# A retention and two-layer MoE kernel: earlier loads in layer 1's accumulators, units from step 4, output products behind the pair

## The chip, the cores and the metric

The kernel runs on one core of a Trainium2 chip. The time is device microseconds of one execution, and of several executions the median is given. The core's engines work side by side, each through its own queue in order: TensorE (PE, with its weight loads PEld), VectorE (DVE), ScalarE (ACT), GpSimd (POOL) and SyncE (SP, which issues most DMAs here).

## What is computed

Eight heads of retention over four batches of 576 tokens, then two dense layers with 2048 inner units over all 2304 tokens. Cut from the reference:

```python
scores = scale * np.matmul(q, k.transpose(0, 1, 3, 2))          # 4 x 8 heads, 576 x 576
gamma = 1.0 - 2.0 ** (-5.0 - np.arange(H, dtype=np.float32))
Dmat = np.where(rel >= 0, gamma[:, None, None] ** rel[None, :, :], 0.0)
attn_out = np.matmul(scores * Dmat[None], v)
x = attn_out.transpose(0, 2, 1, 3).reshape(B * S, H * D)         # 2304 x 512
h = x @ w_in;   x = np.maximum(0.01 * h, h) @ w_out              # layer 1
h = x @ w2_in;  x = (h - np.tanh(h)) @ w2_out                    # layer 2
```

The weights arrive as 64-bit floats.

## The kernel before

**Pairs.** The attention part (`retention`) goes over 16 pairs of heads (4 batches, 4 pairs each), numbered 0 to 15, two heads side by side on 128 partitions. The 576 tokens of a pair are four chunks of 128 and a tail of 64. For a pair, `prep` multiplies q and v with decay tables on POOL, `prep_tail` does the tail of q on VectorE and copies it into a block-diagonal tile `bd` on ScalarE; `scores` are k times q within each chunk (TensorE, into `sc`), `scores_tail` the same for the tail (`x_a`); `mask` applies the decay on VectorE and makes `pt`. `states_mm` makes k times v of each chunk (into `x_c`), and `states` runs the decayed sum over chunks into `st`: a copy on ScalarE and six operations on VectorE, each on the 64 partitions of one head, so that `st` is block-diagonal over 128 columns. One step later `outputs_far` multiplies `st` with q and `outputs_near` multiplies v with `pt`, both into the accumulator `o` and, for the tail, into a part of `x_c`; `finish` splits the result into a high half `xh` (ScalarE) and the rest `xl` (VectorE), which are layer 1's input.

**Narrow units.** Layer 1 begins inside the attention part. Its first group of four f-blocks is done for the first 1536 tokens in 12 units of 256 tokens and two f-blocks: `unit_h` (hidden product, 24 matmuls into `x_b`, then two activations `a` and `g` on ScalarE and a subtraction on POOL), `unit_o` (output product, 24 matmuls into `a`), `unit_evac` (into `acc`, after every second unit). The units' weights are the eight pieces of group 0. A piece is loaded raw (512 KB), narrowed from 64 to 32 bits by five operations (the first, `begin`, on ScalarE, then clamp, shift and two joins `top` and `low` on VectorE, into one of two buffers `cw`), and then split into two parts by `split_piece` (ScalarE, then POOL).

**What sets the order.** All is written in order by hand; each engine runs its own instructions in that order. Step i of the loop holds the load of pair i + 2, `prep` of pair i + 1, scores and mask of pair i, `prep_tail` of pair i + 1, then `pair_steps`. The piece operations are one list `ops`; `at_pair` says how many of them are done by the end of each step, and `fill` puts a third of a step's share at each of three places. SP issues pairs and pieces in the written order; a pair's tiles have three buffers, raw pieces two. In `pair_steps` before, from step 5 on (`first = NP + 1`), stand in a row: hidden product of unit u, output product of unit u - 1, far and near products of pair i - 1, states of pair i. After the loop the last hidden product and two output products follow. Then `layers` does the rest of both layers with `acc` as the accumulator of layer 1.

Of the kernel before, what the change touches and what calls it, by code (L numbers as in the profile page):

```python
# [10 lines left out]
F32 = mybir.dt.float32  # L11
# [22 lines left out]
def retention_moe_moe(  # L34
# [70 lines left out]
    def load_piece(key):  # L105
        m, kind, f = key
        src = ((w1i, w1o), (w2i, w2o))[m][kind][f]
        st = stage.tile([P, 512], I64 if wide else F32, tag="st", name="st")
        nc.sync.dma_start(out=st, in_=src)
        raw[key] = st  # L110
# [200 lines left out]
    def piece_ops(keys, split=True, spare=()):  # L311
# [3 lines left out]
        for j, key in enumerate(keys):  # L315
            part = narrow_ops(key)
            if j + 2 < len(keys):
                part.append(lambda k=keys[j + 2]: load_piece(k))
# [7 lines left out]
    def retention():  # L326
        with ExitStack() as ac:
# [18 lines left out]
            sts = [ak.tile([P, NFULL, P], F32, name=f"st{i}") for i in range(2)]  # L346
            bds = [ak.tile([P, 2, TAIL], F32, name=f"bd{i}") for i in range(2)]
            qk, kv, pts = {}, {}, {}
            order = [(b, p) for b in range(B) for p in range(NP)]

# [4 lines left out]
            def load_qk(i):  # L355
                b, p = order[i]
                t = ap_.tile([P, 2, S], F32, tag="qk", name="qk")
                nc.sync.dma_start(out=t[:, 1, :], in_=qT[b, p])
                nc.sync.dma_start(out=t[:, 0, :], in_=kT[b, p])
                qk[i] = t  # L360

            def load_v(i):
                b, p = order[i]
                t = ap_.tile([P, NFULL + NCH, P], F32, tag="kv", name="kv")
# [94 lines left out]
            def outputs_far(i):  # L459
# [300 lines left out]
```

## Time and profile before

| what | us |
|---|---|
| median of 3 runs (894.61 to 895.62) | 895.46 |
| span of the profiled execution | 893.7 |
| TensorE busy in that span | 868.6 (97%) |
| VectorE busy | 541.6 (61%) |
| ScalarE busy | 378.0 (42%) |
| POOL busy | 421.2 (47%) |
| end of the attention part (first matmul of `layers`) | 166.52 |

The median lies 1.76 us above the span of the profiled execution. The views that follow are stretches (busy time of each engine between two times), the chain of waits (followed back from the last instruction) and the timeline. TensorE's fp32 products appear as two records for each instruction. A form such as `64*128` behind a TensorE instruction is the part of the array, rows by columns, that it uses.

### The profile page before, as it was taken

The numbers are of one execution on the slowest core, as the hardware profiler recorded it, in microseconds if no ns is written. First come the engines' busy times: TensorE is split into PE (matmuls) and PEld (weight loads), VectorE is DVE, ScalarE is ACT, GpSimd is POOL, SyncE is SP. The second block draws the span as 40 slices with busy tenths as digits, with TensorE's granted clock in tenths as the row PEclk, the third lists the DMA queues.
The fourth block names the chain that finished last, engine by engine and source line by source line (L and its number), as shares of the span: only waits on it lengthen the run. The fifth ranks groups of instructions, "written<-read, shape, count | busy, mean of one in ns | idle before, by whom it ended". The sixth has DMA issues, their size and how long they took to land.

```text
span 893.7 us, 13252 instructions
## 1 busy us (share of the span) xinstructions
PE 868.6 (97%) x5024; PEld 747.0 (84%) x5024; DVE 541.6 (61%) x922; ACT 378.0 (42%) x767; POOL 421.2 (47%) x340
## 2 busy tenths in 40 slices
PE   6869999999999999999999999999999999999998
PEld 5759999988888889888888888888888888888886
DVE  6864544698898787865662544444545555555454
ACT  2333232232222321232324666675566555565553
POOL 4544342265223622264224654585457744585443
PEclk9789999999999999999999999999999999999999
DMA  7634432132365335631120200020001000001111
GB/s 276 230 124 131 137 107 101 48 118 95 132 186 166 107 118 157 186 106 47 48 83 24 61 12 1 0 72 24 1 1 43 17 1 1 1 1 48 48 48 70
DMA packets 28574, 70.95 MB, mean 79 GB/s; under 512 B 3296, under 2 KB 3680, under 8 KB 28512
## 3 DMA queue, kind: packets, MB, share of 16 engines
q1 hardware_dynamic: 27936, 69.74, 23.7%
q8 instruction: 39, 0.64, 0.3%
q10 hardware_dynamic: 576, 0.38, 0.1%
q14 instruction: 23, 0.19, 0.1%
HBM read 59.10 MB, written 11.01 MB: 78 GB/s over the span
## 4 chain that ended last, share of the span: by engine, by line
PE 92%; DMA 2%; DVE 2%; POOL 1%; ACT 1%; issue 1%; SPq 0%; POOLq 0%; ACTq 0%
PE h L194 40%; PE a L266 40%; PE a L543 4%; PE x_b L518 3%; DMA kv<-in_vn 2%; PE sc L401 1%; PE o L477 1%; PE o L465 1%; POOL wp L175 1%; PE x_c L434 1%; PE x_a L407 0%; POOL kv L378 0%; DVE cw L148 0%; DVE cw L142 0%; PE x_c L477 0%
## 5 line engine op out<-in xcount | busy, mean ns | idle before, releaser
L194 PE MATMUL h<-xh,wp 128*128 128x512 f32 (+1 forms) x1184 | 355.3, 366 | 0.0
L194 PEld LDWEIGHTS h<-xh,wp 128*128 128x128 f32 x1184 | 216.1, 188 | 36.9
L194 PE MATMUL h<-xl,wp 128*128 128x512 f32 (+1 forms) x592 | 216.9, 366 | 0.0
L266 PE MATMUL a<-wp,g 128*128 128x512 f32 x864 | 209.4, 390 | 0.2 <-POOL g L240 0.2
L266 PEld LDWEIGHTS a<-wp,g 128*128 128x128 f32 x864 | 161.0, 188 | 33.8 <-POOL g L240 1.0
L266 PE MATMUL a<-g,wp 128*128 128x512 f32 (+1 forms) x816 | 175.6, 364 | 0.0
L240 POOL TENSOR_TENSOR g<-v,g 128x512 fp32r<-128x512 f32 (+1 forms) x80 | 94.9, 1186 | 144.6 <-ACT g L239 144.5
L266 PEld LDWEIGHTS a<-g,wp 128*128 128x128 f32 x816 | 141.4, 189 | 24.6
L240 POOL TENSOR_TENSOR g<-a,g 128x512 fp32r<-128x512 f32 (+1 forms) x68 | 87.5, 1286 | 154.5 <-ACT g L208 141.1
L207 ACT ACTIVATE a<-h 128x512 f32<-128x512 f32 (+1 forms) x68 | 37.3, 548 | 227.1 <-PE h L194 226.1
L175 POOL TENSOR_TENSOR wp<-cw,wp 128x512 fp32r<-128x512 f32 x64 | 91.1, 1432 | 82.8 <-ACT wp L174 82.5
L194 PEld LDWEIGHTS h<-xl,wp 128*128 128x128 f32 x592 | 111.6, 189 | 18.6
L233 DVE TENSOR_TENSOR h<-h,t 128x512 f32<-128x512 f32 (+1 forms) x80 | 51.5, 644 | 107.3 <-ACT t L217 107.3
L148 DVE SCALAR_TENSOR_TENSOR cw<-st,cw 128x512 uint32<-128x512 uint32 x128 | 113.3, 885 | 4.0
L292 DVE TENSOR_TENSOR acc<-a,acc 128x512 f32<-128x512 f32 (+1 forms) x114 | 74.0, 662 | 68.3 <-PE a L266 68.1
L239 ACT ACTIVATE g<-v 128x512 fp32r<-128x512 f32 (+1 forms) x80 | 47.2, 589 | 145.4 <-DVE v L237 144.3
L218 POOL TENSOR_TENSOR v<-t,u 128x512 f32<-128x512 f32 (+1 forms) x80 | 94.7, 1184 | 14.2 <-ACT t L217 13.8
L234 DVE SCALAR_TENSOR_TENSOR v<-q,v 128x512 f32<-128x512 f32 (+1 forms) x80 | 55.5, 694 | 55.2 <-POOL v L218 54.2
L237 DVE COPY_PREDICATED v<-mk,h 128x512 f32<-128x512 uint32 (+1 forms) x80 | 54.8, 685 | 9.2 <-DVE v L234 1.4
L219 ACT ACTIVATE q<-u,qb 128x512 f32<-128x512 f32 (+1 forms) x80 | 54.5, 681 | 0.0
L222 ACT ACTIVATE mk<-u,qb 128x512 f32<-128x512 f32 (+1 forms) x80 | 54.2, 678 | 0.0
L131 DVE TENSOR_SCALAR cw<-st 128x512 uint32<-128x512 uint32 x56 | 40.5, 724 | 18.6 <-DMA st<-in_w2i 6.4
(60 smaller groups left out, 803.7 us busy)
## 6 DMA issues: line engine op xcount, KB each, us to landing
st<-in_w1i SPq DMA_DIRECT2D x16, 512.0 KB, 3.3
st<-in_w1o SPq DMA_DIRECT2D x16, 512.0 KB, 3.2
st<-in_w2i SPq DMA_DIRECT2D x16, 512.0 KB, 3.8
st<-in_w2o SPq DMA_DIRECT2D x16, 512.0 KB, 3.8
kept<-cw SPq DMA_DIRECT2D x24, 256.0 KB, 4.1
cw<-kept SPq DMA_DIRECT2D x24, 256.0 KB, 2.6
kv<-in_vn SPq DMA_DIRECT2D x16, 320.0 KB, 5.2
qk<-in_qT SPq DMA_DIRECT2D x16, 288.0 KB, 3.4
```

The lines of the kernel that those rows point to most:

```text
L148: nc.vector.scalar_tensor_tensor(out=t["w"], in0=t[src], scalar=scalar, in1=t["w"], op0=op, op1=ALU.bitwise_or)
L175: nc.gpsimd.tensor_tensor(out=wp[:, 1, :], in0=wf, in1=wp[:, 0, :].bitcast(F32), op=ALU.subtract)
L194: nc.tensor.matmul(out=ps[:, :n], lhsT=w[:, wi, cs], rhs=x[:, kk, t0:t0 + n], start=kk == 0 and i == 0, stop=kk == KK - 1 and i == 2,)
L218: nc.gpsimd.tensor_tensor(out=v[:, :n], in0=t_[:, :n], in1=u[:, :n], op=ALU.mult)
L219: nc.scalar.activation(out=q[:, :n], in_=u[:, :n], func=AF.Square, scale=math.sqrt(RHO_C), bias=qb[:, 0:1])
L222: nc.scalar.activation(out=mk[:, :n], in_=u[:, :n], func=AF.Relu, bias=qb[:, 1:2])
L233: nc.vector.tensor_tensor(out=h, in0=h, in1=t_, op=ALU.subtract)
L234: nc.vector.scalar_tensor_tensor(out=v, in0=q, scalar=RHO_A, in1=v, op0=ALU.add, op1=ALU.mult)
L237: nc.vector.copy_predicated(out=v, mask=mk.bitcast(U32), data=h)
L240: nc.gpsimd.tensor_tensor(out=gt[:, 1, :n], in0=v, in1=gt[:, 0, :n].bitcast(F32), op=ALU.subtract)
L266: nc.tensor.matmul(out=o, lhsT=l, rhs=r, start=f == 0 and i == 0 and d % pack == 0, stop=f == GF - 1 and i == 2 and (d + 1) % pack == 0, s ...
L292: nc.vector.tensor_tensor(out=dst, in0=a, in1=dst, op=ALU.add)
```

## The change

- `load_qk` and `load_v` put pairs 3 and 4 into parts of `acc` (table `homes`), and `load_piece` puts pieces 2 to 5 into other parts of it, so that all of these are queued ahead of the loop without waiting for a buffer. Pair j is then loaded in step i with j = i + 4 for i of 0 and 1 and i + 2 later, where j is over 4: pair 5 in step 1 and, by the same rule, again in step 3, each time into a fresh buffer.
- The pieces come in another order: both of `w_in`, both of `w_out`, for f-blocks 0 and 1, then the same for 2 and 3; `at_pair` is shorter.
- Units start in step 4 (`first = NP`). In `pair_steps` the far and near products of pair i - 1 and its `finish` come first, then the output product of unit u - 1, then the states of pair i, then the hidden product of unit u.
- `st` is 64 columns wide, with both heads on the 128 partitions; `states` is one copy and three operations with a column `decay` as factor; the far products are eight of 64 rows by 64 columns of the array in place of four of 128 by 128.

```diff
-    def load_piece(key):
+    def load_piece(key, at=None):
+        if at is None:
+            st = stage.tile([P, 512], I64 if wide else F32, tag="st", name="st")
+        elif wide:
+            st = acc[:, at:at + 1024].bitcast(I64)
...
-    def piece_ops(keys, split=True, spare=()):
+    def piece_ops(keys, split=True, spare=(), ahead=2):
-            if j + 2 < len(keys):
-                part.append(lambda k=keys[j + 2]: load_piece(k))
+            if j + ahead < len(keys):
+                part.append(lambda k=keys[j + ahead]: load_piece(k))
...
-            sts = [ak.tile([P, NFULL, P], F32, name=f"st{i}") for i in range(2)]
+            sts = [ak.tile([P, NFULL, 64], F32, name=f"st{i}") for i in range(2)]
+            decay = ak.tile([P, NP], F32, name="decay")
+            homes = {3: (4608, 5760), 4: (6912, 8064)}
...
-                for h in range(2):
-                    o = slice(64 * h, 64 * h + 64)
-                    nc.scalar.activation(out=st[o, 0, o], in_=c_[o, 0, :], func=AF.Copy)
+                nc.scalar.activation(out=st[:, 0, :], in_=c_[:, 0, :], func=AF.Copy)
                 for c in range(1, NFULL):
-                    for h in range(2):
-                        o = slice(64 * h, 64 * h + 64)
-                        nc.vector.scalar_tensor_tensor(
-                            out=st[o, c, o], in0=st[o, c - 1, o],
-                            scalar=float(gamma[2 * p + h] ** CH), in1=c_[o, c, :],
-                            op0=ALU.mult, op1=ALU.add,
-                        )
+                    nc.vector.scalar_tensor_tensor(
+                        out=st[:, c, :], in0=st[:, c - 1, :], scalar=decay[:, p:p + 1],
+                        in1=c_[:, c, :], op0=ALU.mult, op1=ALU.add,
+                    )
...
-                    nc.tensor.matmul(
-                        out=dst, lhsT=st[:, c - 1, :], rhs=q[:, cs],
-                        start=c in (1, NFULL), stop=False, skip_group_check=True,
-                    )
+                    for h in range(2):
+                        o = slice(64 * h, 64 * h + 64)
+                        nc.tensor.matmul(
+                            out=dst[o], lhsT=st[o, c - 1, :], rhs=q[o, cs],
+                            start=c in (1, NFULL), stop=False, skip_group_check=True,
+                        )
...
-            pieces = split_order(pieces_of(0, 0))
-            ops = piece_ops(pieces)
-            at_pair = [3, 8, 14, 21, 30, 44, 54]
-            first = NP + 1
+            pieces = [(0, kind, f0 + f) for f0 in (0, 2) for kind in range(2) for f in range(2)]
+            ops = piece_ops(pieces, ahead=6)
+            at_pair = [6, 12, 14, 18, 34, 50]
+            first = NP
...
-            def pair_steps(i, fast):
+            def pair_steps(i):
-                if fast:
-                    unit_h(u)
-                    fill(i, 1)
-                    if u:
-                        unit_o(u - 1)
-                        unit_evac(u - 1)
-                    u += 1
                 if i:
                     ot = outputs_far(i - 1)
                     outputs_near(i - 1, ot, [NFULL])
                     outputs_near(i - 1, ot, range(NFULL))
                     del pts[i - 1], kv[i - 1]
+                    finish(i - 1, ot)
+                if u:
+                    unit_o(u - 1)
+                    unit_evac(u - 1)
+                fill(i, 1)
                 if i < len(order):
                     states_mm(i)
-                if i:
-                    finish(i - 1, ot)
-                if i < len(order):
                     states(i)
+                    if i >= first:
+                        unit_h(u)
+                        u += 1
...
             load_v(0)
-            load_qk(1)
             load_piece(pieces[0])
-            load_v(1)
+            load(1)
+            load_piece(pieces[1])
+            load(2)
+            load(3)
+            load_piece(pieces[2], 0)
+            load_piece(pieces[3], 1024)
+            load(4)
+            load_piece(pieces[4], 2048)
+            load_piece(pieces[5], 3072)
...
-                if i + 2 < len(order):
-                    load(i + 2)
+                j = i + (2 if i > 1 else 4)
+                if 4 < j < len(order):
+                    load(j)
```

**TensorE in a full step, before** (`sc` scores, `x_a` their tail, `x_b` the hidden product, whose other rows are left out, `a` the output product, `o` and `x_c` far and near products, the last `x_c` the states):

```order
L401 MATMUL sc<-qk 128x128 x8
L407 MATMUL x_a<-bd_101,qk 128x128
L518 MATMUL x_b<-xh,wp 128x256
...
L543 MATMUL a<-g,wp 128x256 x24
L465 MATMUL o<-qk,st_100 128x128 x3
L465 MATMUL x_c<-qk,st_100 128x64
L477 MATMUL x_c<-pt,kv 64x64 x2
L477 MATMUL o<-pt,kv 64x128 x8
L434 MATMUL x_c<-kv 64x64 x8
```

**The same step in the changed kernel:**

```order
L420 MATMUL sc<-qk 128x128 x8
L426 MATMUL x_a<-bd_102,qk 128x128
L481 MATMUL o<-qk,st_100 64x128 x6
L481 MATMUL x_c<-qk,st_100 64x64 x2
L493 MATMUL x_c<-pt,kv 64x64 x2
L493 MATMUL o<-pt,kv 64x128 x8
L559 MATMUL a<-g,wp 128x256 x24
L453 MATMUL x_c<-kv 64x64 x8
L534 MATMUL x_b<-xh,wp 128x256
```

The output product now stands between the near products and the states, and the hidden product behind the states; the far products have twice the rows at half the output partitions.

**ScalarE in the step of the first unit, before** (step 5; `cw<-st` is a piece's first narrowing operation, `wp` its split, `bd` the tail copies, `xh` the finish, `st` the state copy, `a` and `g` the unit's two activations):

```order
L127 ACTIVATE cw<-st 128x512
L390 ACTIVATE bd_101<-qk 64x64 x2
L174 ACTIVATE wp<-cw 128x512
L525 ACTIVATE a<-x_b 128x512
L526 ACTIVATE g<-x_b 128x512
L127 ACTIVATE cw<-st 128x512
L174 ACTIVATE wp<-cw 128x512
L486 ACTIVATE xh<-x_c 128x64
L486 ACTIVATE xh<-o 128x512
L444 ACTIVATE st_100<-x_c 64x64 x2
```

**ScalarE in the step of the first unit in the changed kernel** (step 4; raw pieces are read from `acc`):

```order
L409 ACTIVATE bd_103<-qk 64x64 x2
L132 ACTIVATE cw<-acc 128x512
L179 ACTIVATE wp<-cw 128x512
L502 ACTIVATE xh<-x_c 128x64
L502 ACTIVATE xh<-o 128x512
L132 ACTIVATE cw<-acc 128x512
L461 ACTIVATE st_99<-x_c 128x64
L541 ACTIVATE a<-x_b 128x512
L542 ACTIVATE g<-x_b 128x512
L179 ACTIVATE wp<-cw 128x512
L132 ACTIVATE cw<-acc 128x512
```

The unit's two activations moved from ahead of the finish and the state copy to behind them, and a split and the next piece's first operation are queued behind the activations.

**SP's queue behind pair 3's load in the changed kernel** (`acc<-in_w` pieces 2 to 5, `acc<-in_q` pair 4, `st` pieces 6 and 7, `qk` and `kv` pair 5's two loads, the second one cut):

```order
L114 DMA acc<-in_w1o 128x512 x2
L370 DMA acc<-in_qT 128x576
L373 DMA acc<-in_kT 128x576
L384 DMA acc<-in_kn 128x512
L385 DMA acc<-in_vn 128x640
L114 DMA acc<-in_w1i 128x512 x2
L114 DMA st<-in_w1o 128x512
L370 DMA qk<-in_qT 128x576
L373 DMA qk<-in_kT 128x576
L384 DMA kv<-in_kn 128x512
L385 DMA kv<-in_vn 128x640
L114 DMA st<-in_w1o 128x512
```

Before, each piece from the third on stood behind one more pair, and both waited for a free buffer there.

## Rows read from the trace of the kernel before

**Rows 1.** Stretches: length; busy time (count) per engine; granted clock; DMA share, GB/s.
```profile
0.00:79.99 79.99, 58.84 (x608) 53.54 (x609) 55.32 (x140) 27.15 (x71) 37.82 (x33) 0.89 0.58 199
79.99:166.52 86.53, 86.53 (x964) 84.36 (x964) 36.18 (x115) 24.78 (x70) 29.24 (x23) 1.00 0.31 102
```

**Rows 2.** Chain of waits, one step: start us, duration us, engine, tile, line, records.
```profile
85.67 0.67 PE o L465 x6
86.51 0.27 PE x_c L477 x4
86.78 0.88 PE o L477 x16
87.65 0.46 PE x_c L434 x16
88.12 1.09 PE sc L401 x16
89.21 0.42 PE x_a L407 x2
89.63 2.87 PE x_b L518 x24
```

**Rows 3.** Chain of waits, the last step of the attention part.
```profile
155.64 3.06 PE x_b L518 x24
158.71 2.82 PE a L543 x24
...
163.50 3.02 PE a L543 x24
166.52 4.31 PE h L194 x36
```

**Rows 4.** Timeline of TensorE: start, duration, line, operands, array form, shape.
```profile
85.51 0.83 PE L465 MATMUL o<-qk,st 128*128 128x128 f32 x6
...
86.44 0.34 PE L477 MATMUL x_c<-pt,kv 128*64 128x64 f32 x4
...
88.05 1.16 PE L401 MATMUL sc<-qk 64*128 64x128 f32 x16
```

**Rows 5.** Timeline of VectorE: masks of pairs 1 and 4, state operations.
```profile
14.60 1.29 DVE L416 SCALAR_TENSOR_TENSOR pt<-sc,cm_sb 128x512 f32<-128x512 f32 x2
...
36.63 1.29 DVE L416 SCALAR_TENSOR_TENSOR pt<-sc,cm_sb 128x512 f32<-128x512 f32 x2
...
40.90 1.46 DVE L448 SCALAR_TENSOR_TENSOR st<-st,x_c 64x64 f32<-64x64 f32 x6
```

**Rows 6.** Stretches: the first loads, and the first hidden product.
```profile
4.00:14.00 10.00, 7.33 (x56) 6.41 (x57) 4.95 (x15) 1.61 (x6) 5.12 (x4) 1.00 1.01 373
...
39.83:44.08 4.25, 4.25 (x28) 4.25 (x28) 3.77 (x11) 1.42 (x4) 2.34 (x3) 0.70 0.63 227
```

**Rows 7.** Timeline of POOL: two operations that waited for a load to land.
```profile
12.56 1.26 POOL L378 TENSOR_TENSOR kv<-kv,vt_sb 128x640 f32<-128x640 f32 x1 [2.03 <-DMA kv<-in_vn]
...
14.63 1.28 POOL L373 TENSOR_TENSOR qk<-qk,qt_sb 128x512 f32<-128x512 f32 x1 [0.81 <-DMA qk<-in_qT]
```

**Rows 8.** Timeline: a narrowing shift while POOL works, and one without.
```profile
44.07 1.26 POOL L378 TENSOR_TENSOR kv<-kv,vt_sb 128x640 f32<-128x640 f32 x1 [1.87 <-PE x_b L518]
44.18 1.44 DVE L142 TENSOR_SCALAR cw<-cw 128x512 uint32<-128x512 uint32 x1
...
57.75 0.43 DVE L142 TENSOR_SCALAR cw<-cw 128x512 uint32<-128x512 uint32 x1
```

**Rows 9.** Timeline: activation, POOL's split of a unit, first narrowing operation, weight split.
```profile
49.06 0.59 ACT L526 ACTIVATE g<-x_b 128x512 fp32r<-128x512 f32 x1
49.83 1.31 POOL L527 TENSOR_TENSOR g<-a,g 128x512 fp32r<-128x512 f32 x1
49.91 0.68 ACT L127 ACTIVATE cw<-st 128x512 f32<-128x512 f32 x1 [0.27 <-POOL wp L175]
...
50.49 0.62 ACT L174 ACTIVATE wp<-cw 128x512 fp32r<-128x512 f32 x1
```

More of the change, by code (lines that the diff above doesn't have):

```diff
@@ L103, in retention_moe_moe @@
     early = [True]
-    def load_piece(key):
+    def load_piece(key, at=None):
         m, kind, f = key
         src = ((w1i, w1o), (w2i, w2o))[m][kind][f]
-        st = stage.tile([P, 512], I64 if wide else F32, tag="st", name="st")
+        if at is None:
+            st = stage.tile([P, 512], I64 if wide else F32, tag="st", name="st")
+        elif wide:
+            st = acc[:, at:at + 1024].bitcast(I64)
+        else:
+            st = acc[:, at:at + 512]
         nc.sync.dma_start(out=st, in_=src)
@@ L356, in load_qk @@
                 b, p = order[i]
-                t = ap_.tile([P, 2, S], F32, tag="qk", name="qk")
+                if i in homes:
+                    a = homes[i][0]
+                    t = acc[:, a:a + 2 * S].rearrange("p (s t) -> p s t", s=2)
+                else:
+                    t = ap_.tile([P, 2, S], F32, tag="qk", name="qk")
                 nc.sync.dma_start(out=t[:, 1, :], in_=qT[b, p])
+                if i == 0:
+                    nc.scalar.dma_start(out=qt_sb[:, 0, :], in_=qtab[:, 0, :])
                 nc.sync.dma_start(out=t[:, 0, :], in_=kT[b, p])
@@ L363, in load_v @@
                 b, p = order[i]
-                t = ap_.tile([P, NFULL + NCH, P], F32, tag="kv", name="kv")
+                n = NFULL + NCH
+                if i in homes:
+                    a = homes[i][1]
+                    t = acc[:, a:a + n * P].rearrange("p (c d) -> p c d", c=n)
+                else:
+                    t = ap_.tile([P, n, P], F32, tag="kv", name="kv")
                 nc.sync.dma_start(out=t[:, :NFULL, :], in_=kn[b, p])
@@ L574, in pair_steps @@
                     del pts[i - 1], kv[i - 1]
+                    finish(i - 1, ot)
[3 more added lines that the diff above has]
+                fill(i, 1)
                 if i < len(order):
                     states_mm(i)
-                if i:
-                    finish(i - 1, ot)
-                if i < len(order):
                     states(i)
-            t = ap_.tile([P, 2, S], F32, tag="qk", name="qk")
-            nc.sync.dma_start(out=t[:, 1, :], in_=qT[0, 0])
-            nc.scalar.dma_start(out=qt_sb[:, 0, :], in_=qtab[:, 0, :])
-            nc.sync.dma_start(out=t[:, 0, :], in_=kT[0, 0])
-            qk[0] = t
+                    if i >= first:
+                        unit_h(u)
+                        u += 1
+            load_qk(0)
             nc.scalar.dma_start(out=cm_sb, in_=cmask)
@@ L597, in retention @@
             nc.scalar.activation(out=qb[:, 3:4], in_=qb[:, 2:3], func=AF.Tanh)
-            for t in sts + bds:
+            for t in bds:
                 nc.vector.memset(t, 0.0)
-            load_piece(pieces[1])
+            for p in range(NP):
+                for h in range(2):
+                    nc.vector.memset(
+                        decay[64 * h:64 * h + 64, p:p + 1], float(gamma[2 * p + h] ** CH)
+                    )
             prep(0)
@@ L603, in retention @@
             for i in range(len(order)):
-                if i + 2 < len(order):
-                    load(i + 2)
-                fast = i >= first
+                j = i + (2 if i > 1 else 4)
+                if 4 < j < len(order):
+                    load(j)
                 if i + 1 < len(order):
@@ L614, in retention @@
                 fill(i, 0)
-                pair_steps(i, fast)
+                pair_steps(i)
                 fill(i, 2)
-            pair_steps(len(order), True)
+            pair_steps(len(order))
             assert done[0] >= len(ops)
-            unit_o(u - 1)
-            unit_evac(u - 1)
-            assert 2 * u == n_early
+            assert u == n_early // 2
     def layers():
```

## Prediction

> **What bounds the kernel now.** I read the stretches first. From 79.99 us to the end of the attention part at 166.52 us TensorE is busy 86.53 us of 86.53; in the 79.99 us ahead of that it is busy only 58.84 us, at a mean granted clock of 0.89 [rows 1]. After 166.52 us the MoE layers run as before, so the change can only move the moment at which the attention part ends. That moment is set by two things: when TensorE becomes saturated, and how much TensorE time is left then. The chain of waits prices the second, for one pair and one narrow unit [rows 2]: far products 0.67 + 0.17 us (85.67 to 86.51), near 0.27 + 0.88, states 0.46, scores 1.09, their tail 0.42, hidden product of a unit 2.87. The unit's output product takes 2.82 [rows 3]. One step is 9.65 us and nothing waits in it.
>
> **Part 1, units one step earlier.** In the changed kernel the first unit stands in step 4 instead of step 5, so when pair 8's scores are done one unit more is behind it, 5.69 us of TensorE time. I count from a place that both bounds can be tied to: the start of pair 6's scores, t6, which stands right behind the second unit's hidden product. Left from there in the changed order: 10 scores with tail (15.1), 11 far and near (21.9), 10 states (4.6), 10 hidden products (28.7), 11 output products (31.0), together 101.3 us at the prices of rows 2 and 3. So at unchanged prices the attention part would end level with before if t6 = 166.5 - 101.3 = 65.2.
>
> **Part 2, the output products later: form changes.** The profile prints for each TensorE instruction which part of the array it uses: near products and states `128*64`, scores `64*128`, tail, units and old far products `128*128` [rows 4]. Before, a step changes form three times: scores to tail, far to near, states to scores. What stands behind a change costs more than its columns. The tail is two passes that cost 0.11 each in the far products (0.67 for six) but it takes 0.42: 0.20 more. The scores take 1.09, where eight pairs of passes at 0.11 give 0.88: 0.21 more. The first four near passes, of 64 columns, take 0.27 behind the change, where sixteen of 128 columns take 0.88 and four of half the length would take 0.11: 0.16 more. The last step of before holds exactly the two changes that will stand in every step afterwards: the hidden product behind states takes 3.06 instead of 2.87 (155.64), and the output product behind near products takes 3.02 instead of 2.82 (163.50) [rows 3]; where full form follows full form (2.82 at 158.71) nothing is added.
>
> In the changed order a step is scores, tail, far, near, output product, states, hidden product. The far products are now 64 by 64, so tail to far is a change; near to output product, output product to states and states to hidden product are three more. That is 7 changes a step in place of 3. From t6 on: 11 + 11 + 10 + 10 = 42 new ones. Prices: 0.20 and 0.19 read directly for two kinds, 0.16 for the kind that leads from full form into `128*64`; tail to 64 by 64 is in no row, its neighbours are 0.16 to 0.21. I take 0.18 each, 7.6 us; bounds 0.10 (only half of it is lost) and 0.21, 4.2 to 8.8 us. Nothing covers them: TensorE has no idle time there. A step becomes about 10.4 us. The move itself opens no new wait in a full step: between a hidden product and its output product stand scores, tail, far and near products, 3.5 us and two changes, and the two activations and POOL's split take 2.6 [rows 9].
>
> The Trainium skill bears on this in TensorEngine Tiling (Array Packing), Key Properties: changing the tiling mode, and not just the tile, drains TensorE. The rows above agree. It states no price; taken as a rule alone it counts 42 drains against the change, while someone who reads 3.06 and 3.02 as end effects of the last step would have none, and would get the time of the first rival below.
>
> **Part 3, smaller edits on TensorE.** The far products become eight instructions of 64 columns instead of four of 128. Near products, also pairs of half-array instructions, cost 0.11 an instruction, old far ones 0.22; six at 0.11 and two of half the length give 0.78 to 0.93 against 0.84. I take no change (-0.7 to +1.0 us over 11 pairs). That both quarters run at once is in no row; one after the other is a rival. State operations: six of 64 partitions in 1.46 us [rows 5] become three of 128 with a column as factor; the free size is the same, so I take 0.73 us off VectorE per pair, at worst none. This lies behind TensorE later and counts only in steps 1 to 3 (2.2 us). The 1 us of memsets of the states falls away ahead of the first landing, worth nothing. At the end only far and near products (2.2 us) stand there, against the same 2.6: 0.4 us lost. With 0.2 for the second unit's weights I take 0.6.
>
> **Part 4, when t6 comes.** (a) *Landing.* Queued loads run without a pause at 373 GB/s [rows 6]; what POOL waits for lands at 3.5 us + MB queued / 0.365: 3.26 MB at 12.56 and 4.08 MB at 14.63 [rows 7] (by their shapes a pair is 1.18 MB, a piece 0.52, the tables 0.38). The new queue runs on like this, since pairs 3 and 4 and four pieces wait for no buffer. Pair 5's load is written twice in the diff (at i = 1 and, into a fresh buffer, at i = 3), and the second one is used; its first part stands behind 11.95 MB and lands at 36.2 us. The wasted 1.18 MB are 3.2 us of queue. (b) *VectorE.* It starts pair 1's mask at 14.60 and pair 4's at 36.63 now [rows 5]. Between them the changed order has three narrowing operations fewer (2.1 us) and three times 0.73 less, but piece 1's clamp waits behind tail copies and a first operation on ScalarE (about 1.3): 33 to 34.5. Mask and tail take 1.6 and the tail wants pair 5, so at 36.4 us the landing releases it, not VectorE. (c) *Step 4.* From there one chain runs over all engines, each operation at its price in rows 8 and 9 and about 0.05 between them. The queued last narrowing operation of piece 2 collides with POOL's work on pair 5: an operation that meets POOL ends only after it, 1.44 against 0.43 [rows 8]. So 38.2; split on ScalarE 38.9; xh and xl of pair 3 40.4; states 41.2; first hidden product, half of it at half clock as now (4.25 us, mean granted clock 0.70) [rows 6], 45.4; its two activations 46.6; split 3 behind them on ScalarE, and on POOL behind the unit's split, 49.3; only then is the second narrow buffer free for piece 5's first operation 50.0; clamp and shift 50.9; and pair 5's mask is queued behind those. (d) *Step 5.* Mask and tail 52.5, tail copies 53.0, split 4 on ScalarE 53.7 and POOL 55.0, piece 6's first operation 55.7, xh 56.5, split 5 on ScalarE 57.2 and POOL 58.6; then the second half of the second hidden product, 1.45 us, or 2.9 in part at the low clock, because TensorE waited over 4 us: t6 = 60.1 to 62. I take 61.5; with a landing up to 1.5 us either way and one collision more or less, 58.5 to 64.
>
> **Sum.** 61.5 + 101.3 + 7.6 + 0.6 = 171.0 us against 166.5: 4.5 us later. The profiled execution's span of 893.7 becomes 898.2; the median of the runs is 1.76 above that span, so 895.46 becomes 900.0.
>
> **Rivals.**
> *Faster: form changes are free in mid-stream.* Then 61.5 + 101.3 + 0.6 = 163.4, 3.1 us earlier, 892.3 us. It decides below a price of 0.07 us per change (3.1 / 42). For it: two of the direct rows are from the last step. Against it: the scores, tail and near rows of every step show the same 0.16 to 0.21. Chance 0.15.
> *Level: t6 at 58.* The loads land a microsecond earlier, the first units run warm, collisions are missed: 58 + 101.3 + 7.6 + 0.6 = 167.5, and with a price of 0.15 166.2: 895 to 896.5 us. Chance 0.17.
> *Later start.* Split 3 and 5 meet one more queue each and t6 is 65: 174.5, 903.5 us. Chance 0.11.
> *The far quarters do not run at once.* Each at 0.22: +0.66 a pair, 11 pairs, +7.3 on the forecast: 907.3 us. Against it: halves of the array do overlap in the near rows. Chance 0.07.
> *Forecast:* 898 to 902.5 us, chance 0.50.
>
> **How the numbers follow.** A measurement of this kernel can tell about 0.2%, 1.8 us. Slower: 0.50 + 0.11 + 0.07 = 0.68; same 0.17; faster 0.15. The range for 8 in 10 leaves out most of the faster rival below and the serial quarters above: 894.0 to 905.5, which is also t6 of 58.5 at the low price and 64 at the high one, less their corners.
>
> **What would show it.** Right: TensorE saturated from about 62 us, ten steps of about 10.4 us behind that, each hidden product near 3.06 and each output product near 3.02 in the chain, attention ending near 171 us; a wait of VectorE for pair 5's load near 36 us and pair 5's mask near 51 us. Wrong in part 2 if a step is 9.7 us; wrong in part 4 if pair 6's scores start before 58 or after 64 us; wrong in part 3 if the far products take over 1.2 us.

## The result and the profile after

The changed kernel takes 902.82 us, the median of four runs (902.11 to 903.81), beside 895.54 for the kernel before on the same chip: a ratio of 1.0079, interval 1.0065 to 1.0092. It is slower by 7.3 us, where 4.5 were forecast. The profiled execution spans 901.2 us.

The stretches of the changed kernel (columns as in [rows 1], over times of the changed kernel) show the loss inside the attention part:

```profile
0.00:79.99 79.99, 57.63 (x627) 51.77 (x628) 53.66 (x122) 23.80 (x58) 36.73 (x32) 0.87 0.57 206
79.99:173.91 93.92, 93.66 (x1076) 86.25 (x1073) 40.59 (x91) 25.62 (x67) 30.32 (x25) 1.00 0.32 101
24.00:34.00 10.00, 6.60 (x76) 5.76 (x72) 7.27 (x17) 2.50 (x8) 3.29 (x3) 0.67 1.04 398
29.80:31.80 2.00, 2.00 (x18) 1.78 (x17) 0.84 (x3) 0.89 (x2) 0.00 (x0) 0.50 1.03 398
66.47:173.91 107.44, 107.18 (x1242) 98.65 (x1243) 48.85 (x108) 30.88 (x79) 38.52 (x31) 1.00 0.32 99
```

The attention part ends at 173.91 us; before it was 166.52 [rows 1]. That is 7.4 us, so the layers behind it give nothing back. TensorE is saturated from 66.47 us on (107.18 of 107.44), and ahead of that its clock is low in several stretches: 0.67 as the mean from 24 to 34 us, and 0.50 in the 2 us of pair 3's scores, which is the lower of its two levels, 1.2 instead of 2.4 GHz (in what follows, the low clock).

The chain of waits of the changed kernel: the moment t6, a full step, and the end (start, duration, engine, tile, line, records):

```profile
62.15 4.32 PE x_b L534 x24
66.47 1.09 PE sc L420 x16
...
76.70 1.09 PE sc L420 x16
77.79 0.42 PE x_a L426 x2
78.21 0.80 PE o L481 x12
79.01 0.11 PE x_c L481 x4
79.13 0.27 PE x_c L493 x4
79.39 0.88 PE o L493 x16
80.27 2.94 PE a L559 x24
83.20 0.61 PE x_c L453 x16
83.82 3.07 PE x_b L534 x24
86.89 1.09 PE sc L420 x16
...
158.19 1.09 PE sc L420 x16
...
171.01 2.90 PE a L559 x23
173.91 4.30 PE h L199 x36
```

t6, the start of pair 6's scores, is 66.47 us, 5.0 later than forecast. Nine steps lie between there and pair 15's scores at 158.19: 10.19 us each, against 9.65 before. In [rows 2, 3] the same work costs 2.82 (output product), 0.46 (states) and 2.87 (hidden product); now it is 2.94, 0.61 and 3.07. The far products cost 0.80 + 0.11 against 0.67 + 0.17. From t6 to the end are 107.44 us, 6.1 more than the 101.3 of the old prices: nine times 0.54 in the steps, and 1.3 in the last 15.72 us.

VectorE's timeline of the changed kernel shows how t6 came to be late (start, duration, line, operation, operands; in brackets the idle time ahead and what ended it):

```profile
12.10 1.64 DVE L153 SCALAR_TENSOR_TENSOR cw<-st,cw 128x512 uint32<-128x512 uint32 x1
15.71 1.28 DVE L435 SCALAR_TENSOR_TENSOR pt<-sc,cm_sb 128x512 f32<-128x512 f32 x2
20.05 1.50 DVE L147 TENSOR_SCALAR cw<-cw 128x512 uint32<-128x512 uint32 x1
22.29 2.60 DVE L153 SCALAR_TENSOR_TENSOR cw<-st,cw 128x512 uint32<-128x512 uint32 x2
24.82 1.28 DVE L435 SCALAR_TENSOR_TENSOR pt<-sc,cm_sb 128x512 f32<-128x512 f32 x2
30.13 0.92 DVE L463 SCALAR_TENSOR_TENSOR st<-st,decay,x_c 128x64 f32<-128x64 f32 x3 [0.56 <-ACT st L461]
31.89 1.29 DVE L435 SCALAR_TENSOR_TENSOR pt<-sc,cm_sb 128x512 f32<-128x512 f32 x2 [0.85 <-PE sc L420]
38.70 1.28 DVE L435 SCALAR_TENSOR_TENSOR pt<-sc,cm_sb 128x512 f32<-128x512 f32 x2
47.38 1.41 DVE L153 SCALAR_TENSOR_TENSOR cw<-acc,cw 128x512 uint32<-128x512 uint32 x2
53.35 0.79 DVE L142 TENSOR_SCALAR cw<-cw 128x512 f32<-128x512 f32 x1 [4.56 <-ACT cw L132]
55.47 1.28 DVE L435 SCALAR_TENSOR_TENSOR pt<-sc,cm_sb 128x512 f32<-128x512 f32 x2
```

The masks of pairs 1 to 5 start at 15.71, 24.82, 31.89, 38.70 and 55.47 us. Before, pairs 1 and 4 stood at 14.60 and 36.63 [rows 5]. Two joins take 2.60 where two without POOL beside them take 1.41 (47.38). What POOL did then, from its timeline in the changed kernel:

```profile
20.00 1.27 POOL L180 TENSOR_TENSOR wp<-cw,wp 128x512 fp32r<-128x512 f32 x1 [2.51 <-ACT wp L179]
21.23 1.46 POOL L392 TENSOR_TENSOR acc<-acc,qt_sb 128x512 f32<-128x512 f32 x1
22.64 1.71 POOL L397 TENSOR_TENSOR acc<-acc,vt_sb 128x640 f32<-128x640 f32 x1
24.31 1.72 POOL L392 TENSOR_TENSOR acc<-acc,qt_sb 128x512 f32<-128x512 f32 x1
26.15 1.26 POOL L397 TENSOR_TENSOR acc<-acc,vt_sb 128x640 f32<-128x640 f32 x1
```

Pairs 3 and 4, which lie ready in `acc`, are prepared in one go beside the joins of the second piece, and not each in its step. The shift of 1.50 us (20.05) stands beside POOL's split of the first piece.

### The profile page after: what moved, and what is told of

Its sections match the earlier page's. It is cut to its first block, busy times and chain, and to the rows that moved or that the text cites. A ratio compares the mean times of both kernels' runs of the same rounds, so it can differ in the third digit from the quotient of the medians.

```text
span 901.2 us, 13450 instructions
## 1 busy us (share of the span) xinstructions
PE 874.5 (97%) x5152; PEld 747.1 (83%) x5152; DVE 545.9 (61%) x880; ACT 375.7 (42%) x751; POOL 421.2 (47%) x340
## 4 chain that ended last, share of the span: by engine, by line
PE 92%; issue 3%; POOL 2%; DVE 1%; DMA 1%; ACT 1%; SPq 0%; POOLq 0%; ACTq 0%
PE h L199 40%; PE a L271 40%; PE x_b L534 4%; PE a L559 4%; PE sc L420 1%; PE o L481 1%; PE o L493 1%; PE x_c L453 1%; DMA qk<-in_qT 1%; PE x_a L426 1%; DMA qt_sb<-in_qtab 0%; POOL acc L392 0%; POOL acc L397 0%; DVE cw L153 0%; POOL wp L180 0%
## 5 line engine op out<-in xcount | busy, mean ns | idle before, releaser
L153 DVE SCALAR_TENSOR_TENSOR cw<-st,cw 128x512 uint32<-128x512 uint32 x120 | 109.2, 910 | 3.8
L297 DVE TENSOR_TENSOR acc<-a,acc 128x512 f32<-128x512 f32 (+1 forms) x114 | 73.6, 662 | 62.2 <-PE a L271 62.2
L136 DVE TENSOR_SCALAR cw<-st 128x512 uint32<-128x512 uint32 x56 | 38.0, 679 | 23.4 <-DMA st<-in_w2o 7.6
```

Of the source, the lines that this page charges most:

```text
L153: nc.vector.scalar_tensor_tensor(out=t["w"], in0=t[src], scalar=scalar, in1=t["w"], op0=op, op1=ALU.bitwise_or)
L297: nc.vector.tensor_tensor(out=dst, in0=a, in1=dst, op=ALU.add)
```

## The experiments

Each was timed in turn with the kernel before. The end of the attention part is the start of `layers`' first product, and t6 is the start of pair 6's scores; both come from one profiled execution of each kernel, and the time is the median of several.

**The order, taken back.** `e1_old_order` is the changed kernel with the old `pair_steps` and units from step 5.

```diff
-            first = NP
+            first = NP + 1
...
+                if fast:
+                    unit_h(u)
+                    fill(i, 1)
+                    if u:
+                        unit_o(u - 1)
+                        unit_evac(u - 1)
+                    u += 1
                 if i:
                     ot = outputs_far(i - 1)
...
-                    if i >= first:
-                        unit_h(u)
-                        u += 1
...
```

> The changed kernel with the row order of before inside a step (hidden product, output product, far and near products, states; units again from step 5, last two output products behind the loop); loads, pieces, 64-column states and far products stay as changed. Theory A (the new order pays for form changes of the array): a full step falls from 10.19 to about 9.7 us, because only the change ahead of the 64 by 64 far products is left over; the attention part ends near 165 to 168 us in place of 173.9; median 893 to 898 us. Theory B (the order costs nothing and only the late start does): a step stays near 10.2 or the loss of one unit at the start (5.7 us) shows in full; 903 to 908 us.

Measured: 897.98 us, ratio 1.0031 (1.0014 to 1.0048), attention part's end at 169.66. Its chain:

```profile
81.59 1.09 PE sc L420 x16
82.68 0.42 PE x_a L426 x2
83.10 2.88 PE x_b L534 x24
85.98 2.74 PE a L559 x24
88.72 0.80 PE o L481 x12
89.52 0.11 PE x_c L481 x4
...
91.24 1.09 PE sc L420 x16
```

A step is 9.65 us again, with the new far products in it. So 4.8 of the 7.3 us are the order with its earlier unit. The other 2.4 us (1.3 to 4.3 by the interval) are what the rest of the change costs: the new loads, the new order of the pieces and the shorter `at_pair`, less what the cheaper state operations gain. No run takes these apart in the old order. The end came later than the 165 to 168 us that were expected.

**The order alone.** `e2_new_order` gives the kernel before the new `pair_steps`, units still from step 5, all else as before.

```diff
...
+                if u:
+                    unit_o(u - 1)
+                    unit_evac(u - 1)
+                fill(i, 1)
                 if i < len(order):
+                    states_mm(i)
                     states(i)
+                if i >= first:
+                    unit_h(u)
+                    u += 1
...
```

> The kernel before with nothing but the new order inside a step (far and near products, finish, output product, states, hidden product; units from step 5, the last hidden product directly ahead of the last output product). Far products stay in full form. Theory A: three form changes more in each full step (output product behind near +0.12, states behind output product +0.15, hidden product behind states +0.20 as in the changed kernel's chain): step 10.1 us in place of 9.65, over some nine full steps +4.2, and +2.6 at the end where the last output product waits for the split of its own unit: about 902 us (900.5 to 903.5). Theory B (changes free): step 9.65, only the end: 898 us.

Measured: 906.32 us, ratio 1.0115 (1.009 to 1.014), end at 179.27. Pair 7's scores start at 71.87 and pair 15's at 153.61: eight steps of 10.22 us. With full-form far products a step has six form changes instead of three, so 0.57 / 3 = 0.19 each. The time was missed: 4.2 us were expected in the steps and 2.6 at the end, 902 us. In the profiled execution, the slowest of the four, pair 7's scores start 3.8 us later than before (71.87 against 68.03), for which nothing had been expected; the steps from there to pair 15's scores add 3.8, and the end adds 5.1 (25.66 us from those scores on, against 20.59). At the end, with the last unit's hidden product behind everything, its output product waits for ScalarE and POOL (1.24 and 1.02 us idle) and then runs at the low clock:

```profile
173.60 0.38 PE L543 MATMUL a<-g,wp 128*128 128x256 f32 x1 [1.24 <-ACT g L526]
175.00 4.27 PE L543 MATMUL a<-g,wp 128*128 128x256 f32 x23 [1.02 <-POOL g L527]
```

In the changed kernel, where the units start in step 4, this end has only 0.26 us of idle time. That end is one thing that the earlier unit buys.

**Form changes by themselves.** `e6_states_between` is the kernel before, with the states put between hidden and output product from step 8 on: two more changes a step and nothing else.

```diff
                     fill(i, 1)
+                    if 8 <= i < len(order):
+                        states_mm(i)
                     if u:
...
-                if i < len(order):
+                if i < min(8, len(order)):
                     states_mm(i)
```

> The kernel before with the states' products of pairs 8 to 15 moved to between a step's hidden and output product; nothing else. All of it lies in the saturated part, and each of eight steps gets exactly two form changes more (full form into 128*64 and back). Theory A (a change costs 0.12 to 0.20 us wherever it stands): +0.3 a step, +2.4 us, 898 us (897 to 898.6), the output product in the chain 2.94 to 3.02 in place of 2.82. Theory B (the price belongs to the start or end of a unit or to another wait): 895.5 us, step 9.65.

Measured: 898.58 us, ratio 1.0038 (1.0024 to 1.0052), end at 169.56, 3.0 later. The chain:

```profile
113.00 0.62 PE x_c L434 x16
113.62 3.05 PE a L543 x24
```

Four steps from pair 9's scores take 40.04 us (88.52 to 128.56), 10.01 each: 0.18 a change. This settles the first rival: a form change costs as much in mid-stream as at the end.

**Far products and state operations.** `e3_far_full` is the changed kernel with six state operations and far products over the whole array.

```diff
...
-                    for h in range(2):
-                        o = slice(64 * h, 64 * h + 64)
-                        nc.tensor.matmul(
-                            out=dst[o], lhsT=st[o, c - 1, :], rhs=q[o, cs],
+                    nc.tensor.matmul(
+                        out=dst, lhsT=st[:, c - 1, :], rhs=q[:, cs],
...
```

> The changed kernel with the states of before (six operations on a block-diagonal tile of 128 columns, far products in full form). Theory A: far products 0.84 in place of 0.91 us a pair, -0.8 us over 11 pairs in the saturated part; state operations 1.46 in place of 0.92 on VectorE, +0.5 in each of steps 0 to 2, where VectorE and POOL set the pace, +1.6: together 903.6 us (902 to 905). If the early state operations lie behind other waits: 902.0 us.

Measured: 904.57 us, ratio 1.0102 (1.0083 to 1.012). Pair 7's scores start at 77.27 and pair 15's at 158.18, 10.11 us a step with six changes, 0.15 each. `e2_new_order` has the same products in a step of 10.22 us: its output product takes 3.04 us and this one 2.94, and why is open. The attention part of `e3_far_full` ends at 174.08, 0.2 later than in the changed kernel; the medians differ by 1.75 us, and the intervals overlap. The smaller state tile gains a little at the start (pair 7's scores 0.6 us earlier) and gives 0.08 back in each step.

**The second load of pair 5.** `e5_one_load` loads it once.

```diff
-                j = i + (2 if i > 1 else 4)
-                if 4 < j < len(order):
+                j = i + 2
+                if i > 2 and j < len(order):
```

> The changed kernel with pair 5 loaded once (step 3) instead of twice; nothing else is different. Theory A (VectorE and POOL, not the load queue, release step 4 and 5): the 1.18 MB that go are worth nothing, 902 to 903.5 us, pair 6's scores at 66 to 67 us. Theory B (the queue sets the start, and part of the gain of the pairs in the ring was the load that went with them): 1.18 MB at 0.39 MB per us are 3.0 us, so 899.5 to 900.5 us and pair 6's scores at 63 to 64 us.

Measured: 902.59 us, ratio 1.0079 (1.0063 to 1.0095): no difference from the changed kernel. Pair 6's scores start at 65.96. The queue doesn't set the start.

**Pairs 3 and 4 through the ring of buffers.** `e9_ring_pairs` leaves the pieces in `acc`, and loads the pairs in the steps as before.

```diff
-            homes = {3: (4608, 5760), 4: (6912, 8064)}
+            homes = {}
...
-            load(3)
...
-            load(4)
...
-                j = i + (2 if i > 1 else 4)
-                if 4 < j < len(order):
+                j = i + 2
+                if 2 < j < len(order):
```

> The changed kernel with pairs 3 and 4 loaded into the ring of three buffers again (load of pair i + 2 in step i, no pair loaded twice); the four raw pieces stay in the accumulators. Theory A (early loads let POOL prepare pairs 3 and 4 back to back, which collides with VectorE's narrowing in steps 1 and 2): the long joins (1.50, 2.60) and the tail (1.21) of 20 to 28 us shrink, pair 2's mask starts 1 to 2 us before 24.82, median 901 to 902.5 us. Theory B (the early loads are what keeps the start from being later still): pair 3's or 4's preparation waits for a landing, median 904 to 906 us.

Measured: 899.55 us, ratio 1.0045 (1.003 to 1.006), t6 62.98, end at 170.50: a gain of 3.3 us, more than expected, and by the run before it none of it is the load that goes too. VectorE's timeline of it:

```profile
20.89 1.41 DVE L153 SCALAR_TENSOR_TENSOR cw<-st,cw 128x512 uint32<-128x512 uint32 x2
22.21 1.28 DVE L435 SCALAR_TENSOR_TENSOR pt<-sc,cm_sb 128x512 f32<-128x512 f32 x2
...
28.08 1.29 DVE L435 SCALAR_TENSOR_TENSOR pt<-sc,cm_sb 128x512 f32<-128x512 f32 x2 [0.28 <-PE sc L420]
```

POOL now waits 4.62 us for pair 3 and starts on it at 24.49. The joins of the second piece have no POOL operation beside them (1.41 against 2.60), and pair 3's mask starts at 28.08 instead of 31.89: a pair that lies ready early takes POOL into the time of the narrowing. These joins take 1.41 or 1.42 us in all three kernels that load the pairs through the ring (this one, `e11_all_start` and `e13_old_order_start`), and 2.60 to 3.31 in all six that have them early. But of the 3.8 us at pair 3's mask, 1.4 stand at pair 1's already (14.34 against 15.71), ahead of these joins: there a join of the first piece starts at 12.06, just ahead of POOL's product at 12.13, and takes 0.69, where in the changed kernel it starts at 12.10 behind POOL's at 11.93 and takes 1.64. `e11_all_start`, with the pairs in the ring too, has 1.66 there, so this part is not shown to come from the ring. That pieces 2 to 5 also land earlier in this kernel was not tried apart.

**A third narrow buffer.** `e4_three_narrow` changes one number.

```diff
-            cw_pool[0] = ac.enter_context(tc.tile_pool(name="c0", bufs=2))
+            cw_pool[0] = ac.enter_context(tc.tile_pool(name="c0", bufs=3))
```

> The changed kernel with three buffers for narrowed pieces in place of two. Theory A (the start is late through the chain in which a piece's first operation on ScalarE waits for POOL's split two pieces back): the waits of VectorE ahead of the clamps shrink (4.56 at 53.35, 1.94 at 60.41), pair 6's scores start at 62.5 to 64.5 us in place of 66.47, median 899.5 to 901 us. Theory B (the start is set by the first hidden product and the collisions of VectorE with POOL alone): pair 6's scores within 0.5 us of 66.5, 902.8 us.

Measured: 900.54 us, ratio 1.0059 (1.0041 to 1.0077), t6 64.53, end at 171.97. The first operation of piece 5 no longer waits for POOL's split (2.09 us in the changed kernel, start 52.64), but starts at 51.27 in the chain, behind ScalarE's own split. Pair 5's mask starts at 53.73. The forecast's chain through the two buffers existed, and was worth 1.9 us.

**Products without use in TensorE's waits.** `e8_warm` puts 16, 22 and 30 of them into the waits of steps 2, 4 and 5.

```diff
+                    if i in (2, 4):
+                        warm(16 if i == 2 else 22)
                     finish(i - 1, ot)
...
+                    if i == 5:
+                        warm(30)
```

> The changed kernel with added matmuls whose result nobody reads (16, 22 and 30 of 256 columns into the hidden accumulator, in the waits of TensorE in steps 2, 4 and 5, behind the near products and behind the first output product). Theory A (low clock is part of the late start): scores of pair 3 from 2.08 to about 1.2 us, first hidden product from 4.56 to about 3, second from 4.32 to about 3, pair 6's scores at 62.5 to 64.5 in place of 66.47, 899.5 to 901 us. Theory B (the start is set by VectorE, ScalarE and POOL alone): 902.8 us, or later by what the added products hold up.

Measured: 899.12 us, ratio 1.0039 (1.0024 to 1.0053), end at 169.97. Its chain:

```profile
41.20 0.69 PE x_c L453 x16
41.89 3.08 PE x_b L534 x24
...
57.98 4.36 PE x_b L534 x24
62.34 1.09 PE sc L420 x16
```

The first hidden product takes 3.08 instead of 4.56 us, pair 3's scores 1.16 instead of 2.08, and t6 is 62.34. The second hidden product still takes 4.36: the 30 products ahead of it ended at 55.0, and TensorE idled until 57.1. So 3.7 us of the loss come back when the waits of the start are filled; the two groups of products at the full clock account for 2.4 of the 4.1 us of t6. Not all of the rest is the clock: VectorE's tail of pair 3 misses POOL in this trace and takes 0.21 us instead of 1.21, and it does so in `e5_one_load` too, which has no such products.

**All three at once, in the new order and in the old one.** `e11_all_start` joins the edits of `e9_ring_pairs`, `e4_three_narrow` and `e8_warm`. `e13_old_order_start` is `e1_old_order` with the same edits, without the products of step 5:

```diff
+                    if i in (2, 4):
+                        warm(16 if i == 2 else 22)
...
-            cw_pool[0] = ac.enter_context(tc.tile_pool(name="c0", bufs=2))
+            cw_pool[0] = ac.enter_context(tc.tile_pool(name="c0", bufs=3))
-            homes = {3: (4608, 5760), 4: (6912, 8064)}
+            homes = {}
...
```

> The changed kernel with all three repairs of its start together: pairs 3 and 4 through the three ring buffers, a third narrow buffer, and products without use in TensorE's waits of steps 2, 4 and 5. The new order stays. Theory A (the new order costs 107.4 us from pair 6's scores on, whatever the start; the repairs gained 3.5, 1.9 and 4.1 us of start one by one and add in most part): pair 6's scores at 57.5 to 59.5 us, attention part's end 165 to 167, 894 to 896 us, level with the kernel before. Theory B (the repairs cover the same waits): pair 6's scores at 61 to 62.5 us, 897.5 to 899 us.

> The changed kernel with the old order of units and pair products (units from step 5) and the repairs of the start: pairs 3 and 4 through the ring, a third narrow buffer, products without use in TensorE's waits of steps 2 and 4. Theory A (steps of 9.65 instead of 10.2 us, ten of them, are worth more than the unit that starts one step earlier once the start is repaired in both): 890 to 893 us, 2 to 4 us below the same repairs under the new order. Theory B (with an early start the new order gives back its form changes, since TensorE works through step 4): 895 to 898 us, 1 to 3 us above the new order with the same repairs.

Measured: new order 895.02 us, ratio 0.9998 (0.9988 to 1.0008), t6 59.4, end at 167.33. Old order 892.71 us, ratio 0.9967 (0.9956 to 0.9979), end at 163.37. With 7 us less of start the new order is level with the kernel before, and the last 108.0 us are 0.5 more than they were: in step 6 TensorE now waits for a split of weights. The old order, from step 5 on, is still 2.3 us shorter.

**The useful parts on the kernel before.** `e7_before_states_three` takes the three state operations, the 64 by 64 far products (both as in the diff of the change) and a third narrow buffer into the kernel before; `e12_first_output_later` moves one output product in one step of that. First the one edit, then the other:

```diff
-            cw_pool[0] = ac.enter_context(tc.tile_pool(name="c0", bufs=2))
+            cw_pool[0] = ac.enter_context(tc.tile_pool(name="c0", bufs=3))
...
-            sts = [ak.tile([P, NFULL, P], F32, name=f"st{i}") for i in range(2)]
+            sts = [ak.tile([P, NFULL, 64], F32, name=f"st{i}") for i in range(2)]
...
+                    nc.vector.scalar_tensor_tensor(
+                        out=st[:, c, :], in0=st[:, c - 1, :], scalar=decay[:, p:p + 1],
+                        in1=c_[:, c, :], op0=ALU.mult, op1=ALU.add,
+                    )
...
```

```diff
                     fill(i, 1)
-                    if u:
+                    if u > 1:
                         unit_o(u - 1)
...
                     states_mm(i)
+                if i == first + 1:
+                    unit_o(0)
+                    unit_evac(0)
```

> The kernel before with the three state operations on 64 columns (and far products of 64 by 64) and, in the room that this frees, three buffers for narrowed pieces; order, loads and pieces as before. From the old-order run, far products of 64 by 64 behind an output product leave a step at 9.65 us. Theory A: the start gets 0.5 us a step shorter on VectorE and loses waits on POOL's splits: 2 us faster than before, 893.5 us (892.3 to 894.7). Theory B: the start is set by TensorE's cold units and the landing: 895.5 us.

> The kernel before with three state operations, 64 by 64 far products and a third narrow buffer, and in step 6 alone the first unit's output product behind the states instead of ahead of the far products, so that far and near products and states run while its weights are still being split. Theory A (TensorE's wait of 4.9 us ahead of that product's second half sets the start, and 2.5 us of other work now lies in it): 2 to 3 us less than without the move, 889.5 to 890.5 us. Theory B (pair 6's mask and VectorE set the steps behind it, so the wait only moves): 891.5 to 893 us.

Measured: 892.40 us, ratio 0.997 (0.996 to 0.9981), end at 165.61; and 888.95 us, ratio 0.992 (0.99 to 0.9941), end at 161.13, a little below what was expected. The kernel before took 895.23 and 895.76 beside them; the profiled execution of the first is its slowest, 2.4 us above its median, so the profiles lie further apart than the times. TensorE's timeline, first without the move, then with it:

```profile
59.34 0.79 PE L541 MATMUL a<-g,wp 128*128 128x256 f32 x2 [4.90 <-ACT wp L174]
60.69 2.50 PE L541 MATMUL a<-g,wp 128*128 128x256 f32 x10 [0.55 <-POOL wp L175]
```

```profile
54.18 0.87 PE L463 MATMUL o<-qk,st 64*64 64x128 f32 x12 [1.36 <-DVE xl L485]
59.11 0.51 PE L541 MATMUL a<-g,wp 128*128 128x256 f32 x2 [0.70 <-ACT wp L174]
60.46 1.79 PE L541 MATMUL a<-g,wp 128*128 128x256 f32 x10 [0.84 <-POOL wp L175]
```

The weights come at the same time, but far products, near products and states are done by then, and pair 6's scores start at 62.2 instead of 67.4. The later output product, the core of the change, pays in the one step in which TensorE waits for its weights, and costs form changes in the ten in which it doesn't. This version is 0.8% faster than the kernel before and 1.5% faster than the changed one.

## Why the prediction was right, and where it was not

The sign and the range held (900.0, range 894.0 to 905.5; measured 902.82, which is 0.3 us above the 898 to 902.5 that had a chance of one half). The attention part ended at 173.91 instead of 171.0. The 2.9 us between are a start that came 5.0 us later than forecast, less 2.1 us of TensorE work that was forecast too dear: two errors of opposite sign, so the time is nearer than its terms, and that is luck.

**Part 1** held: the end is t6 plus the work left, in the changed kernel and in `e11_all_start`, 107.4 and 108.0 us behind t6s that differ by 7.

**Part 2** held in mechanism and price, and was off in count. 0.18 us a change was taken; the direct runs gave 0.18 (`e6_states_between`), 0.19 (`e2_new_order`) and 0.15 (`e3_far_full`), and the changed kernel against `e1_old_order` 0.54 for three. Of the four new changes a step, the one ahead of the far products, taken together with their new form, costs far less: 0.08 in the changed kernel against `e3_far_full` (10.19 and 10.11), and nothing in `e1_old_order`, which has that one change more than the kernel before and a step of 9.65 us (its far products take 0.07 more, the output product ahead of them 0.08 less). The term of 7.6 us counted eleven such changes at the full price; at 31 it would have been 5.6, and 5.5 was measured if the forecast 0.6 at the end is left as it was. A step is 10.19, not 10.4. The Trainium skill, TensorEngine Tiling (Array Packing), Key Properties, says that a change of the tiling mode drains TensorE; the runs agree (10.01 against 9.65 us for two changes), and the price is theirs.

**Part 3.** The far quarters do run at once: 0.91 with a change in it, far below the 1.2 that would have shown the serial rival. The state operations were mis-sized: three take 0.92, not 0.73, 0.30 each where one of 64 partitions took 0.24 [rows 5]. In steps 1 to 3 that is 0.6 us less gain.

**Part 4** is the part that failed, outside its own bounds of 58.5 to 64. By its steps:

| place | forecast | measured |
|---|---|---|
| pair 4's mask | 33 to 34.5 | 38.70 |
| tail of pair 5 behind it | 36.4 | 40.16 |
| end of the states of pair 4 | 41.2 | 44.35 |
| end of the first hidden product | 45.4 | 48.91 |
| first operation of piece 5 | 49.3 | 52.64 |
| pair 5's mask | 50.9 | 55.47 |
| t6 | 61.5 | 66.47 |

*(a)* named the wrong releaser. Nothing on VectorE waited for a landing there: the loads ran at up to 398 GB/s, not 373, and 1.18 MB less in the queue changed nothing. *(b)* is the step that failed. VectorE was to reach pair 4's mask at 33 to 34.5 us by taking away what the change removes from steps 1 to 3. It got there at 38.70, and the tail behind it, which was to wait for its load until 36.4, came 3.8 us late: most of the 5.0 us. The operations left did not keep their duration. Pair 1's mask is 1.1 us late already (15.71 against 14.60), behind joins of the first piece that met POOL's work on pairs 1 and 2 (1.64 and 1.30 us for 0.69). POOL's preparation of pairs 3 and 4 moved beside the joins of the second piece (2.60 for 1.41), its split of the first piece stood beside a shift (1.50 for 0.43), and TensorE, after 3.40 us of waiting, ran pair 3's scores at the low clock, for which VectorE then waited 0.85. The price of a collision was known [rows 8], and (c) used it, but only in step 4. *(c)* had the chain right, link by link, and kept its length up to the first operation of piece 5, which came 3.3 us late; then clamp and shift ahead of the mask ran beside POOL (0.79 and 1.37), and pair 5's mask was 4.6 us late. *(d)* had offered 1.45 us or up to 2.9 for half of the second hidden product; behind 5.60 us of waiting the whole of it ran in one piece, the first half of it at the low clock, and took 4.32.

The rival "later start" (t6 65, 903.5 us) was the nearest in time and in t6, though not by its cause: split 3 met the one queue that the forecast had (POOL at 51.34, behind the unit's split at 50.11), split 5 met none (POOL at 61.57, as soon as ScalarE's half was done), and 3.8 us were lost ahead of both. The third buffer takes away a wait that the forecast had (2.09 us), and gives back 1.9. The level rival has its run in `e11_all_start`: with t6 at 59.4, where the level was worked out for 58, the time is 895.02 us. The first rival, free changes, fell with `e6_states_between`. Of the 7.3 us, 4.8 are the new order, net of its earlier unit, and 2.4 the rest of the change, which shows in the start and was not taken apart. The repairs of the start (3.3, 2.3 and 3.7 us by time) overlap: together they gave 7.8.

## What to carry to other kernels

Price a reordering on a saturated TensorE by the changes of array form that it adds to each step, from the excess of instructions that already stand behind a change; then use the new order only in the step that has a wait to fill. Data that arrives earlier also moves the work that prepares it: ask which operations of another engine it will now stand beside, and give them the collided duration, in every step that it passes. When a start gets longer waits on TensorE, price the products behind each wait for the greater part at the low clock: the first hidden product took 4.56 us here and 5.24 in `e4_three_narrow`, against 3.08 with its wait filled.

## What the runs showed of the hardware

A form change cost 0.15 to 0.19 us on a TensorE that is otherwise never idle (`e3_far_full`, `e6_states_between`, `e2_new_order`); the one ahead of the quarter-array far products, with their new form, 0 to 0.08. Two joins on VectorE took 2.60 us beside POOL's products and 1.41 without. A join that started 0.07 us ahead of a POOL product took 0.69 us, and POOL's product then 1.73; one that started 0.17 us behind it took 1.64, and POOL's product 1.26. A hidden product of 24 records took 4.56 us behind 4.2 us of TensorE idling, at a granted clock of 0.62, and 3.08 where products without use filled most of that idling; thirty such products that ended 2 us ahead of the next one left that one at 4.36. Queued loads of the changed kernel ran at 387 GB/s from 4 to 14 us and at 398 in the next two stretches of 10 us, where the kernel before had shown 373 from 4 to 14. A state operation on 128 partitions with a column of factors takes 0.30 us, and 0.24 on 64 partitions with a constant, at the same 64 columns.
